# Attention followed by two gated layers: reciprocals fetched by two transfers of 64 partitions, tails of Q and K loaded per batch, zero columns beside the last keys, a new operation list

## The chip, the core and the metric

The kernel runs on one core of a Trainium2 chip. The metric is the device time of one execution in microseconds (us). Each engine (PE for matmuls, ACT, DVE and POOL for elementwise work) works off its own queue in order; SP issues nearly all DMAs, also in order. Engines wait for one another by semaphores.

## What is computed

```python
scores = scale * q @ k.T                     # 4 batches x 8 heads, 576 rows, head_dim 64
cum = cumsum(max(s, 0))
bias = min(-(cum[:, None] - cum[None, :]), 0)
attn = exp(where(causal, -1e9, scores + bias) - max)
x = (attn / (attn.sum(-1) + 1e-9)) @ v       # -> [2304 tokens, 512]
x = (sigmoid(x @ w_gate) * (x @ w_val)) @ w_out      # d_ff 1536
h = x @ w_in;  out = (h * cos(h)) @ w_out2           # d_ff 2048
```

## The kernel before

The heads go through in 16 pairs p = 0..15, four pairs j to a batch. The operations of a pair have short names, and the text `SEQ` at the top of the file lists all operations of all pairs in one order; `plan.run(SEQ)` walks through the list, picks buffers by planned times and emits each operation on its engine, so the order in `SEQ` is the order in each engine's queue. A letter behind a colon picks the engine (a ACT, d DVE, p POOL).

- GQ, GK, GV load Q, K (512 rows of each head, L515) and V (L574); GQT, GKT load the last 64 rows (L522, L525). Before the change GQT and GKT run for every second pair and bring the tails of two pairs (four heads) into the one buffer `Qt` or `Kt`, the other half of whose partitions was set to zero at the start.
- PQ, PK transpose them on PE (L546); HQ, HK copy the result to SBUF.
- DB brings the cumulated sums of a pair to all partitions (`CB`, L554, 576 KB). ZT, ZA, Z, ZM on POOL set masked biases.
- A are score matmuls (L618, L623), X adds the bias and takes the row maximum on DVE (L654), E is the exponential on ACT (L658), T transposes the result on PE (L444), C copies it (`pt`), V is the product with V on PE (L728, L730), U copies that to `w` (L433 or L437).
- The denominators take another way. RA adds 1e-9 on POOL (L737), RC takes the reciprocal on DVE (L740), RT transposes it on PE, RR copies it to `rr`, RD stores it to DRAM by two small DMAs (L749, L750), RB reads it back spread over all partitions into `rb` (L753, 288 KB), M multiplies `w` by `rb` (L759), XH and XL split the product in two parts for the next stage (L771). There is one `rb` and one `rr`: RB of a pair waits for M of the pair before it.
- w0, w1, w2 decode the first weight pieces; I0 to I7 are the first gate and value matmuls of the next stage.

Behind the list, `moe()` runs the two layers on PE without a break. Its first work on PE is gate and value of the second token block (needs only early batches), then the first down projection, which waits for `gh` on ACT (L826 sigmoid, L829). The memory of `tm` and `gh` is that of the attention's tiles, so these wait until the attention's last operations, XL of pair 15 among them, are through.

```python
def spread(u, p=p):                                              # RB, L753
    u.dma_start(out=RBT, in_=rec_d[p].unsqueeze(1).to_broadcast([2, 64, S]))
add(f"RB{p}", {"sp": 0.62}, spread, rd=[("rec", p)], wr=[rb], xfer=0.9)
```

Of the kernel before, what the change touches and what calls it, by code (L numbers as in the profile page):

```python
# [170 lines left out]
GQ0 cum tail B0 B1 GK0 GQT0 GKT0 out PQ0 table GK1 GQ1 BC0:d BC1:a Z0.0:p PK0 ZM0.3.0 HK0:a HQ0:d PK1 ZT0.0 Z1.0:a A3.0 DB1 ZT1.0 X0.3.0 ZA1.0 ZM1.3.0 ZA0.0 X1.3.0 HK1:a  # L171
PQ1 A4.0 ZM1.2.0 A0.0 GK2 A2.0 ZM0.2.0 HQ1:a ZT1.1 GK3 E0.3.0 GQ2 A4.1 X1.1.0 ZT0.1 X1.0.0 ZA1.1 X0.0.0 ZA0.1 Z1.1:p E1.3.0 Z0.1:p GQ3 X0.1.0 X1.2.0 ZM1.3.1 E1.1.0 X0.2.0
ZM0.3.1 E1.0.0 A0.1 E0.0.0 T0.0.0 E0.1.0 X1.0.1 T0.1.0 X1.1.1 X0.0.1 E1.2.0 X0.1.1 C0.1.0:d C0.0.0:a E0.1.1 A5.0 E0.0.1 A3.1 T0.3.0 GKT2 E1.0.1 X0.4.0 E1.1.1 T1.3.0 GQT2
T0.0.1 E0.4.0 X0.3.1 X1.3.1 T0.1.1 C0.0.1:a PK2 C0.3.0:a HK2:a ZM1.2.1 C1.3.0:d ZM0.2.1 A5.1 C0.1.1:d DB2 E0.2.0 T0.4.0 PQ2 ZT1.2 PK3 GV1 X0.4.1 A2.1 HQ2:a PQ3 GV0 E0.4.1
C0.4.0:d HQ3:a ZA1.2 T0.2.0 HK3:d ZT0.2 T1.2.0 A4.2 T0.4.1 X0.2.1 X1.2.1 A0.2 C0.4.1:d GQ4 ZA0.2 X1.0.2 C0.2.0:a Z1.2:p GQ6 X0.1.2 C1.2.0:a A3.2 E0.3.1 E1.3.1 E1.2.1 RA0
E1.0.2 T0.3.1 ZM1.3.2 X1.1.2 E0.1.2 Z0.2:p T1.3.1 X0.0.2 DB3 E0.2.1 X1.3.2 C1.3.1:a ZM0.3.2 C0.3.1:d RC0 GKT4 GK4 Z0.3:p V0.0 V1.0 T0.2.1 E0.0.2 X0.3.2 ZM1.2.2 E1.1.2
ZM0.3.3 T0.1.2 T0.0.2 T1.2.1 U0:a A5.2 Z1.3:p C0.0.2:d C0.2.1:d C0.1.2:a A2.2 C1.2.1:a ZT0.3 PK4 ZT1.3 A3.3 X0.4.2 X1.2.2 E0.3.2 GQT4 E1.3.2 ZM1.3.3 T0.3.2 ZM0.2.2 X0.2.2
HK4:a T1.3.2 GK5 ZA0.3 C1.3.2:a RT0 X0.3.3 E1.2.2 DB4 V0.1 ZM0.2.3 RR0:d V1.1 RA1 C0.3.2:d E0.4.2 T0.4.2 PQ4 X1.3.3 RC1 ZM1.2.3 RD0 ZA1.3 A4.3 U1:d HQ4:d GK6 A0.3 GV2
E0.2.2 ZT1.4 X1.0.3 X0.0.3 X0.1.3 E0.3.3 Z0.4:p E1.3.3 GV4 RT1 C0.4.2:a ZT0.4 RR1:a Z1.4:p ZA1.4 E1.0.3 E0.0.3 E0.1.3 A2.3 T0.2.2 ZA0.4 X1.1.3 T1.2.2 X0.2.3 A3.4 X1.2.3
RA2 E1.1.3 ZM1.3.4 C1.2.2:a RB0 T0.0.3 T0.1.3 A5.3 RC2 C0.0.3:a C0.2.2:d ZM0.3.4 C0.1.3:a PK5 RD1 HK5:a GQ5 X0.3.4 DB5 M0:p X0.4.3 warm0 RT2 T0.3.3 T1.3.3 RR2:d RB1  # L180
X1.3.4 A4.4 E0.4.3 C0.3.3:a C1.3.3:a ZM0.2.4 RD2 E1.2.3 T0.4.3 Z0.5:p A0.4 Z1.5:p E0.2.3 C0.4.3:d PQ5 X0.0.4 X1.0.4 X1.1.4 V0.2 GKT6 X0.1.4 V1.2 ZT1.5 HQ5:d T0.2.3 RA3
E1.0.4 ZT0.5 E1.3.4 XH0:p E1.1.4 E0.3.4 A2.4 E0.1.4 T1.2.3 U2:a E0.0.4 RC3 C1.2.3:a T0.1.4 C0.2.3:d X0.2.4 C0.1.4:a ZM0.3.5 T0.0.4 ZM1.2.4 A5.4 T0.3.4 GQT6 C0.0.4:a
# [37 lines left out]
def kernel(  # L220
# [168 lines left out]
    def attention():  # L389
        with ExitStack() as c2:  # L390
# [671 lines left out]
```

## Time and profile before

| | us |
|---|---|
| median of 3 runs (lowest, highest) | 1097.45 (1096.66, 1099.25) |
| the profiled execution | 1097.39 |
| its span, first to last instruction | 1095.5 |
| PE busy in the span | 1032.2 (94%) |
| DVE, ACT, POOL busy | 706.5, 477.8, 406.6 |

In slices of a fortieth of the span (27.4 us) the page shows PE at 7 to 8 tenths in the attention, and at 9 or more from the tenth slice on; the granted clock of PE is 8 to 9 tenths in the attention and full after it. The mean busy share of the 16 DMA engines is 3 to 6 tenths in the attention, then 1 to 2. A busy share is an average; what a change is worth is read from the waits of the stage it touches.

### The profile page before, as it was taken

Reading aid. Unit: us, or ns where it says so; the run is one execution under the profiler, and the core shown is the slowest. Engines: PE = TensorE matmul, PEld = TensorE weight load, DVE = VectorE, ACT = ScalarE, POOL = GpSimd, SP = SyncE. Lnnn points to the kernel's source line nnn. Section 1 sums busy time; section 2 is a strip of 40 time slices with the busy share of each in tenths; the row PEclk is TensorE's granted clock in tenths of the full one; section 3 lists DMA queues with packets and bytes.
Section 4 is the critical chain, followed back from the end, with each engine's and each line's share of the span. In section 5 each row is a group of like instructions: output and inputs, shape, how many; then the busy total and the mean of one; then the engine's idle time right before and its main releaser. Section 6 shows DMA issues by size and latency. Waiting matters only on the chain.

```text
span 1095.5 us, 17441 instructions
## 1 busy us (share of the span) xinstructions
PE 1032.2 (94%) x6554; PEld 932.9 (85%) x6554; DVE 706.5 (64%) x1366; ACT 477.8 (44%) x1079; POOL 406.6 (37%) x484
## 2 busy tenths in 40 slices
PE   8778768859999999999999999999999999999998
PEld 5555445539999999999999999999999999999997
DVE  5656546536665564775434488898778978885664
ACT  5757657614422221222212134566555555555443
POOL 3345545424322122232111122465435545453222
PEclk9989888978999999999999999999999999999999
DMA  6645445303211111111101012111101101100111
GB/s 165 158 120 160 131 117 147 82 31 103 71 39 48 50 39 39 59 61 55 39 21 39 20 58 58 40 58 58 39 20 59 58 20 42 56 20 1 58 51 65
DMA packets 93668, 69.94 MB, mean 64 GB/s; under 512 B 61008, under 2 KB 81872, under 8 KB 93584
## 3 DMA queue, kind: packets, MB, share of 16 engines
q1 hardware_dynamic: 92192, 68.43, 21.6%
q8 instruction: 51, 0.84, 0.3%
q10 hardware_dynamic: 1392, 0.40, 0.2%
q14 instruction: 33, 0.27, 0.1%
HBM read 63.95 MB, written 4.87 MB: 63 GB/s over the span
## 4 chain that ended last, share of the span: by engine, by line
PE 77%; DVE 0%; ACT 0%; DVEq 0%; issue 0%
PE pw L356 20%; PE pw L355 20%; PE pw L357 20%; PE pw L909 6%; PE pw L911 6%; PE pw L910 6%; DVE acc L927 0%; ACT gh L829 0%; DVEq L1057 0%
## 5 line engine op out<-in xcount | busy, mean ns | idle before, releaser
L355 PE MATMUL pw<-XH,wp 128*128 128x384 f32 x960 | 322.9, 336 | 1.0 <-DVE w L437 1.0
L357 PE MATMUL pw<-XH,wp 128*128 128x384 f32 x960 | 322.7, 336 | 0.0
L356 PE MATMUL pw<-XL,wp 128*128 128x384 f32 x960 | 322.7, 336 | 0.0
L310 POOL TENSOR_TENSOR wp<-wm,wp 128x512 fp32r<-128x512 f32 x68 | 100.9, 1485 | 228.9 <-DVE wp L309 226.3
L355 PEld LDWEIGHTS pw<-XH,wp 128*128 128x128 f32 x960 | 180.3, 188 | 5.3 <-DVE w L437 1.1
L356 PEld LDWEIGHTS pw<-XL,wp 128*128 128x128 f32 x960 | 180.1, 188 | 3.6
L357 PEld LDWEIGHTS pw<-XH,wp 128*128 128x128 f32 x960 | 180.1, 188 | 0.0
L899 POOL TENSOR_TENSOR gl<-tm,gh 128x384 fp32r<-128x384 f32 x96 | 109.2, 1137 | 143.8 <-ACT gh L898 143.7
L302 POOL TENSOR_TENSOR wm<-wm,wx 128x512 int32<-128x512 int32 x68 | 90.3, 1328 | 188.6 <-DVE wm L301 182.3
L827 DVE TENSOR_TENSOR tm<-pw,tm 128x384 f32<-128x384 f32 x72 | 40.1, 557 | 150.7 <-PE pw L357 139.1
L909 PE MATMUL pw<-wp,gh 128*128 128x512 f32 x288 | 112.2, 389 | 0.0
L910 PE MATMUL pw<-wp,gh 128*128 128x512 f32 x288 | 112.1, 389 | 0.0
L911 PE MATMUL pw<-wp,gl 128*128 128x512 f32 x288 | 112.1, 389 | 0.0
L355 PE MATMUL pw<-gh,wp 128*128 128x384 f32 x288 | 97.5, 339 | 7.9 <-ACT gh L829 7.9
L884 DVE SCALAR_TENSOR_TENSOR tm<-tm 128x384 f32<-128x384 int32 x96 | 98.2, 1023 | 3.3
L829 ACT CAST gh<-tm 128x384 fp32r<-128x384 f32 x72 | 37.0, 514 | 140.8 <-DVE tm L827 139.9
L356 PE MATMUL pw<-gl,wp 128*128 128x384 f32 x288 | 97.8, 340 | 0.0
L885 ACT ACTIVATE tm<-tm 128x384 f32<-128x384 f32 x96 | 50.5, 526 | 108.0 <-DVE tm L884 108.0
L357 PE MATMUL pw<-gh,wp 128*128 128x384 f32 x288 | 96.9, 337 | 0.0
L289 ACT ACTIVATE wx<-wx,ebias 128x512 int32<-128x512 int32 x68 | 49.2, 723 | 105.5 <-DVE wx L288 104.3
L658 ACT ACTIVATE pu<-pu,nm 128x512 f32<-128x512 f32 (+4 forms) x144 | 83.0, 579 | 10.5 <-POOL pu L437 6.2
L826 ACT ACTIVATE tm<-pw 128x384 f32<-128x384 f32 x72 | 35.1, 487 | 111.8 <-PE pw L357 95.8
(100 smaller groups left out, 1673.4 us busy)
## 6 DMA issues: line engine op xcount, KB each, us to landing
raw<-in_moe_w_out_dram SPq DMA_DIRECT2D x28, 512.0 KB
CB<-cum_d SPq DMA_DIRECT2D x15, 576.0 KB
raw<-in_moe_w_in_dram SPq DMA_DIRECT2D x16, 512.0 KB
raw<-in_moe_w_gate_dram SPq DMA_DIRECT2D x12, 512.0 KB
raw<-in_moe_w_val_dram SPq DMA_DIRECT2D x12, 512.0 KB
VN<-in_v_dram SPq DMA_DIRECT2D x31, 160.0 KB
rb<-rec_d SPq DMA_DIRECT2D x16, 288.0 KB
out_dram<-acc SPq DMA_DIRECT2D x17, 256.0 KB
```

The source lines that it names most:

```text
L302: pool.tensor_tensor(m, m, st["x"], ALU.add)
L310: pool.tensor_tensor(w[:, 1], m, f(w[:, 0]), ALU.subtract)
L355: pe.matmul(ps, wh, xh, start=first, stop=False)
L356: pe.matmul(ps, wh, xl, start=False, stop=False)
L357: pe.matmul(ps, wl, xh, start=False, stop=last)
L658: act.activation(o, o, AF.Exp, bias=NMT[nm.slot][:, col:col + 1], scale=-1.0, accum_out=SUMS[sums.slot][:, col:col + 1])
L884: dve.scalar_tensor_tensor(r, kk, -TWO_PI_LO, r, ALU.mult, ALU.add)
L885: act.activation(r, r, AF.Sin, scale=0.5)
L899: pool.tensor_tensor(gl, g, f(gh), ALU.subtract)
L909: pe.matmul(ps, gh[:, ts], w[:, 0], start=it["first"], stop=False)
L910: pe.matmul(ps, gh[:, ts], w[:, 1], start=False, stop=False)
L911: pe.matmul(ps, gl[:, ts], w[:, 0], start=False, stop=it["last"])
```

## The change

- **Spread of the reciprocals.** RB issues two DMAs, one for each head of the pair, each from 576 numbers in DRAM to 64 partitions of `rb`. Before, one DMA with an outer dimension of 2 filled all 128.
- **Tails.** GQT and GKT run for the first pair of a batch and bring the tails of all eight heads; there are two buffers each. K's tails now stand in partitions 64 to 127, so that in the transposed K the last keys stand behind the others, not ahead of them.
- **Zero columns.** The probability tile of the last 64 query rows is 640 columns wide; columns 576 to 639 are set to zero once, so that T of that tile transposes five plain blocks of 128.
- **Start.** Six small warming matmuls (`warm0`) stand before the first real ones, six (`warm1`) behind the first transposes; before, both stood late in the list. The store of the cumulated sums on ACT's queue goes behind the activation table's load.
- **List.** `SEQ` is new throughout, and the planned durations are changed in some places (SP's part of RB from 0.62 to 1.16, T of the small tiles, and others). `moe()` is not touched.

```diff
-GQ0 cum tail B0 B1 GK0 GQT0 GKT0 out PQ0 table GK1 GQ1 BC0:d BC1:a Z0.0:p PK0 ...
+tail cum GQ0 warm0 GKT0 B1 B0 GQT0 PQ0 table GK0 out BC0:a BC1:a GQ1 ZT0.0 PK0 ...
-            QKT = {x: att.tile([P, 2, 2, D], F32, name=f"{x}t") for x in "QK"}
+            QKT = {x: [att.tile([P, PB, 2, D], F32, name=f"{x}t{i}") for i in range(2)] for x in "QK"}
-            PU.append([att.tile([P, S], F32, name=f"pu4{i}") for i in range(NPU[4])])
+            PU.append([att.tile([P, NQ * P], F32, name=f"pu4{i}") for i in range(NPU[4])])
...
-                for e in range(2):
-                    u.memset(QKT["Q"][half(1 - e), :, e], 0.0)
-                u.memset(QKT["K"][half(1)], 0.0)
+                for i in range(2):
+                    for e in range(2):
+                        u.memset(QKT["Q"][i][half(1 - e), :, e], 0.0)
+                    u.memset(QKT["K"][i][half(0)], 0.0)
+                for i in range(NPU[4]):
+                    u.memset(PU[4][i][:, S:NQ * P], 0.0)
...
-            add("out", "act:500", setup_out, rd=["cum"], wr=["cum_d"], xfer=0.2)
+            add("out", "act:400", setup_out, rd=["cum", "table"], wr=["cum_d"], xfer=0.2)
...
-                    if p % 2 == 0:
-                        def load_tail(u, x=x, src=src[b, 2 * j:2 * j + 4, NT4 * P:S]):
+                    if j == 0:
+                        def load_tail(u, x=x, src=src[b, :, NT4 * P:S], tb=tb):
...
-                                u.dma_start(out=QKT[x][half(e), :, e], in_=src[e:e + 3:2].rearrange("h p d -> p h d"))
+                                u.dma_start(out=QKT[x][tb.slot][half(e), :, e], in_=src[e::2].rearrange("h p d -> p h d"))
...
-                                        i = (TAIL + c * P) % S if t == NT4 else c * P
+                                        i = c * P
...
-                    u.dma_start(out=RBT, in_=rec_d[p].unsqueeze(1).to_broadcast([2, 64, S]))
+                    for e in range(2):
+                        u.dma_start(out=RBT[half(e)], in_=rec_d[p, e].unsqueeze(0).to_broadcast([64, S]))
...
-                add(f"RB{p}", {"sp": 0.62}, spread, rd=[("rec", p)], wr=[rb], xfer=0.9)
+                add(f"RB{p}", {"sp": 1.16}, spread, rd=[("rec", p)], wr=[rb], xfer=0.9)
```

How the instructions stand at two places. The first is SP's queue around the first RB. Before, from the loads of V ahead of it to the second RB:

```order
L574 DMA VN_85<-in_v_dram 128x5x64 x2
L753 DMA rb<-rec_d 128x1x576
L749 DMA rec_d<-rr 2x4x128
L750 DMA rec_d<-rr 2x1x64
L515 DMA Qn_87<-in_q_dram 128x4x64 x2
L554 DMA CB_84<-cum_d 128x2x576
L753 DMA rb<-rec_d 128x1x576
```

And now:

```order
L580 DMA VN_85<-in_v_dram 128x5x64 x2
L762 DMA rb<-rec_d 64x576 x2
L757 DMA rec_d<-rr 2x4x128
L758 DMA rec_d<-rr 2x1x64
L560 DMA CB_83<-cum_d 128x2x576
L521 DMA Qn_88<-in_q_dram 128x4x64 x2
L521 DMA Qn_87<-in_q_dram 128x4x64 x2
L762 DMA rb<-rec_d 64x576 x2
```

Each RB has become two rows of 64 partitions, and the loads between two RBs have moved; the stores of `rr` (RD) have kept their shape.

The second place is the end of the attention on ACT, from the last exponential to the first sigmoid of the next stage. Before:

```order
L658 ACTIVATE pu_106,sums_111<-pu_106,nm_114 128x576
L433 COPY pt_94<-pw 128x2x128 x2
L433 COPY pt_94<-pw 128x3x128
L433 COPY pt_94<-pw 128x4x128
L826 ACT_TABLE_LOAD
L826 ACTIVATE tm<-pw 128x384
L829 CAST gh<-tm 128x384
```

And now:

```order
L666 ACTIVATE pu_105,sums_113<-pu_105,nm_116 128x512
L433 COPY pt_96<-pw 128x3x128 x2
L433 COPY pt_96<-pw 128x4x128 x2
L433 COPY w_110<-pw 128x576
L433 CAST XH<-w_111 128x576
L835 ACT_TABLE_LOAD
L835 ACTIVATE tm<-pw 128x384
L838 CAST gh<-tm 128x384
```

U of pair 14 (`w_110`) and XH of pair 15 are now ACT's and stand ahead of the table load and the sigmoid; before, they were on DVE and POOL. XL of pair 14, M and XL of pair 15 are POOL's last three instructions of the attention now; before, M and XL of pair 15 were DVE's.

## Rows read from the trace of the kernel before

**Rows 1.** Windows by stage: length, busy PE, PEld, DVE, ACT, POOL; clock, DMA share, GB/s.
```profile
20.00:48.80 28.80, 26.90 (x356) 18.47 (x352) 20.39 (x65) 24.71 (x74) 11.97 (x39) 0.94 0.63 154
48.80:220.00 171.20, 130.89 (x1463) 87.76 (x1458) 92.87 (x293) 108.25 (x322) 86.17 (x179) 0.89 0.48 127
220.00:248.00 28.00, 13.43 (x77) 8.21 (x75) 10.17 (x18) 2.87 (x4) 8.32 (x8) 0.77 0.08 29
248.00:1095.50 847.50, 843.71 (x4560) 808.62 (x4560) 572.61 (x955) 332.52 (x658) 292.16 (x226) 1.00 0.15 47
```

**Rows 2.** Waits of PE, 20 to 220 us: total us, times, longest.
```profile
PE pw L546 <- DMA Qt<-in_q_dram: 7.1, 2, 4.3
PE pw L728 <- DMA VN<-in_v_dram: 5.5, 4, 2.9
PE pw L444 <- DVE rr L437: 5.1, 1, 5.1
PE pw L444 <- ACT rr L433: 4.8, 2, 4.6
PE pw L546 <- DMA Qn<-in_q_dram: 4.7, 1, 4.7
...
PE pw L546 <- DVE nm L654: 3.1, 2, 2.9
```

**Rows 3.** Windows: a load of CB (first), a load of rb (second).
```profile
191.00:193.20 2.20, 2.20 (x20) 0.90 (x18) 1.76 (x10) 2.20 (x11) 0.24 (x1) 1.00 0.75 276
235.00:241.50 6.50, 4.43 (x24) 4.11 (x24) 1.62 (x3) 0.00 (x0) 1.29 (x1) 1.00 0.12 45
```

**Rows 4.** Timeline: M of pair 13, RB and M of pair 15.
```profile
223.34 1.40 POOL L759 TENSOR_TENSOR w<-w,rb 128x576 f32<-128x576 f32 x1 [8.54 <-DMA rb<-rec_d]
...
233.63 0.50 SPq L753 DMA_DIRECT2D rb<-rec_d  x1
...
242.02 0.76 DVE L759 TENSOR_TENSOR w<-w,rb 128x576 f32<-128x576 f32 x1 [5.39 <-DMA rb<-rec_d]
```

**Rows 5.** Waits, 0 to 250 us: of POOL, and of SP's queue.
```profile
POOL w L759 <- DMA rb<-rec_d: 54.3, 12, 8.5
...
SPq L753 <- DMA rec_d<-rr: 20.0, 10, 5.6
```

**Rows 6.** Timeline: a store of rr and its waiter; an RB, the loads of Q behind it.
```profile
45.44 0.58 SPq L750 DMA_DIRECT2D rec_d<-rr  x1
...
54.18 0.28 DVE L437 COPY rr<-pw 9x128 f32<-9x128 f32 x1 [6.09 <-DMA rec_d<-rr]
...
70.39 0.56 SPq L753 DMA_DIRECT2D rb<-rec_d  x1
71.00 1.24 SPq L515 DMA_DIRECT2D Qn<-in_q_dram  x2
```

**Rows 7.** Lines of ACT (first), then timeline, from 226 us to the first down projection.
```profile
L433 ACT COPY w<-pw 128x576 f32<-128x576 f32 x5 | 3.1, 628 | 0.9 <-PE pw L730 0.9
...
226.19 0.28 PE L444 MATMUL pw<-ident,rc 64*9 64x64 f32 x2 [5.76 <-DVE rc L740]
...
228.82 1.28 ACT L826 ACT_TABLE_LOAD   x1
...
232.00 2.76 PE L730 MATMUL pw<-pt,VN 128*64 128x512 f32 x20
...
246.00 1.41 POOL L771 TENSOR_TENSOR XL<-w,XH 128x576 fp32r<-128x576 f32 x1
246.08 0.49 ACT L826 ACTIVATE tm<-pw 128x384 f32<-128x384 f32 x1 [15.97 <-POOL wp L310]
246.60 0.56 DVE L827 TENSOR_TENSOR tm<-pw,tm 128x384 f32<-128x384 f32 x1 [1.96 <-ACT tm L826]
...
247.44 0.51 ACT L829 CAST gh<-tm 128x384 fp32r<-128x384 f32 x1 [0.87 <-POOL XL L771]
...
248.00 0.69 PE L355 MATMUL pw<-gh,wp 128*128 128x384 f32 x1 [7.86 <-ACT gh L829]
```

More of the change, by code (lines that the diff above doesn't have):

```diff
@@ L213 @@
-M12:p I0 E0.0.15 X1.2.15 XH11:a X0.2.15 I1 E1.1.15 I2 RC14 RB13 E1.0.15 E0.1.15 T0.1.15 XH12:a M13:p E0.2.15 E1.2.15 RT14 RR14:d T0.0.15 A5.15 T0.4.14 XH13:p X0.4.15 I3
-C0.0.15:a I4 GV15 RD14 I5 E0.4.15 C0.4.14:d C0.1.15:a T0.4.15 T0.2.15 T1.2.15 T0.3.15 C1.2.15:d T1.3.15 C0.4.15:d C0.2.15:a I6 RA15 RB14 RC15 w2mant_hi I7 RT15 C1.3.15:d
-C0.3.15:a V0.14 V1.14 XL13:d RR15:d V0.15 w2mant_lo XL11:d V1.15 U14:d M14:d U15:d RD15 XL12:p XH14:d RB15 w2sign M15:d XH15:p XL15:d w2split XL14:p
+tail cum GQ0 warm0 GKT0 B1 B0 GQT0 PQ0 table GK0 out BC0:a BC1:a GQ1 ZT0.0 PK0 GK1 warm1 Z0.0:p HQ0:a ZT1.0 Z1.0:p DB1 ZM0.3.0 PQ1 ZA0.0 HK0:d A3.0 ZM1.3.0 ZA1.0 X0.3.0
@@ L416, in attention @@
             pl = {n: Pool(c) for n, c in dict(
-                Q=NQK, K=NQK, Qt=1, Kt=1, cc=NCC, vn=NV, pt=NPT, w=NW, rb=1, sums=3, nm=3, rc=1, rr=1, raw=1,
+                Q=NQK, K=NQK, Qt=2, Kt=2, cc=NCC, vn=NV, pt=NPT, w=NW, rb=1, sums=3, nm=3, rc=1, rr=1, raw=1,
                 cb=NCC, **{f"pu{t}": NPU[t] for t in range(NQ)},
@@ L447, in attention @@
             zero = PU[4][1].bitcast(BF16)[:, 0:512]
-            ss, cs, one = WT[0][0:NH], WT[1][0:NH], PU[4][0][0:NH]
+            ss, cs, one = WT[0][0:NH], WT[1][0:NH], PU[4][0][0:NH, 0:S]
             sp.dma_start(out=ss, in_=s.rearrange("b h s -> (b h) s"))
@@ L492, in warm @@
                         pe.matmul(PW[:, wm.slot, 0:2 * P], one_b[:, 0:P], one_b, start=z == 0, stop=z == 5)
-                add(f"warm{i}", "pe:650", warm, rd=["z"], wr=[wm, "z"], at=3.9)
+                if i == 0:
+                    add("warm0", "pe:1200", warm, wr=[wm, "begin"], at=3.9)
+                else:
+                    warm1 = warm, wm
             def geom(t):
@@ L544, in prep @@
                                     o = o[:, i:i + D]
[L545 removed]
+                                i = QKN[x][qk.slot][half(h), c] if c < NT4 else QKT[x][tb.slot][half(h), j]
                                 pe.transpose(o, i.rearrange("p e d -> p (e d)"), ident[half(h), half(h)])
[L547 removed]
+                    add(f"P{x}{p}", "pe:380", prep, rd=[(qk, 0), (qk, 1), tb] + ["begin"] * (p == 0), wr=[ps] + [("turned", x)] * (p == 0))
                     def keep(u, x=x, ps=ps, cc=cc):
@@ L555, in attention @@
                 if p:
-                    add(f"DB{p}", {"sp": 0.55}, spread_cum, rd=["cum_d"], wr=[(cb, e, 0) for e in range(2)], xfer=2.1)
+                    add(f"DB{p}", {"sp": 0.45}, spread_cum, rd=["cum_d"], wr=[(cb, e, 0) for e in range(2)], xfer=2.1)
                 else:
@@ L577, in attention @@
                 add(f"GV{p}", {"sp": 1.05}, load_v, rd=[], wr=[vn], xfer=1.4)
-                ready = [(cc, x) for x in "QK"]
+                if p == 0:
+                    add("warm1", "pe:700", warm1[0], rd=[("turned", x) for x in "QK"], wr=[warm1[1], "go"])
+                ready = [(cc, x) for x in "QK"] + ["go"] * (p == 0)
                 first, late = [], []
@@ L622, in scores4 @@
                             z = e ^ turn
-                            pe.matmul(PW[:, sc[0].slot + z, 0:HS], OPS["Q"][cc.slot][half(e), QCOL[NT4]:QCOL[NT4] + P], OPS["K"][cc.slot][half(e), z * HS:(z + 1) * HS], start=turn == 0, stop=turn == 1)
+                            pe.matmul(PW[:, sc[0].slot + z, 0:HS], OPS["Q"][cc.slot][half(e), QCOL[NT4]:QCOL[NT4] + P], OPS["K"][cc.slot][half(e), TAIL + z * HS:TAIL + (z + 1) * HS], start=turn == 0, stop=turn == 1)
                     groups[g] = ts, s4, pus, pu_of, sc, at, bias
@@ L627, in attention @@
                         parts = [lambda u, turn=turn, scores4=scores4: scores4(u, turn) for turn in range(2)]
-                        add(f"A4.{p}", "pe:480", parts[0], rd=ready, wr=[sc[0], ("a4", p)], needs=[pus[NT4][0]])
+                        add(f"A4.{p}", "pe:500", parts[0], rd=ready, wr=[sc[0], ("a4", p)], needs=[pus[NT4][0]])
                         sc4 = sc[0]
                     else:
-                        add(f"A{g}.{p}", f"pe:{ {0: 660, 2: 640, 3: 850}[g] }", scores, rd=ready + [("a3" if g == 2 else "a4", p)] * (g != 3), wr=sc[:1] + ([("a3", p)] if g == 3 else [("a0", p)] if g == 0 else []), needs=[pus[t][0] for t in ts])
+                        add(f"A{g}.{p}", f"pe:{ {0: 720, 2: 670, 3: 870}[g] }", scores, rd=ready + [("a3" if g == 2 else "a4", p)] * (g != 3), wr=sc[:1] + ([("a3", p)] if g == 3 else [("a0", p)] if g == 0 else []), needs=[pus[t][0] for t in ts])
                 for e in range(2):
@@ L635, in bias4_tail @@
                     def bias4_tail(u, e=e, cb=cb, pu=pu):
-                        later(u, PU[NT4][pu.slot][half(e), 0:TAIL], CB[cb.slot][:, e][half(e), NT4 * P:S])
+                        later(u, PU[NT4][pu.slot][half(e), NT4 * P:S], CB[cb.slot][half(e), e, NT4 * P:S])
                     def bias4(u, e=e, cb=cb, pu=pu):
-                        copy(u, PU[NT4][pu.slot][half(e), TAIL:S], CB[cb.slot][half(e), e, 0:NT4 * P])
+                        copy(u, PU[NT4][pu.slot][half(e), 0:NT4 * P], CB[cb.slot][half(e), e, 0:NT4 * P])
                     add(f"ZT{e}.{p}", "pool:180", bias4_tail, rd=[(cb, e, 0)], wr=[(pu, e, "t"), ("z4", p, e)])
                     add(f"ZA{e}.{p}", "pool:490", first[e], rd=[(cb, e, 0), ("z4", p, e)], wr=[(cb, e, 2)])
-                    add(f"Z{e}.{p}", "pool:562 act:470", bias4, rd=[(cb, e, 0)], wr=[(pu, e, "c"), ("z5", p, e)])
+                    add(f"Z{e}.{p}", "pool:562 act:640", bias4, rd=[(cb, e, 0)], wr=[(pu, e, "c"), ("z5", p, e)])
                 for g, (ts, s4, pus, pu_of, sc, at, bias) in ((g, groups[g]) for g in (3, 2, 0, 4)):
```

104 lines of the change are left out of this document (52 added, 52 removed).

## The prediction

> **What bounds the kernel now.** I read the windows by stage first. From 248.0 us on, PE is busy for 843.7 of 847.5 us at full clock [rows 1]: the two layers are bound by PE, the change doesn't touch them, and they should take the same 847.5 us from the moment when their first down projection starts (248.00, [rows 7]). So the question is when that start comes. The profiled execution took 1097.4 us, 1.9 more than its span and 0.05 below the median of the runs, so a shift of the start is taken off 1097.4 as it stands.
>
> Ahead of that start lie three stretches. From 20 to 48.8 us, before the first reciprocals have come in, PE is busy 26.90 of 28.80 us at a granted clock of 0.94 and works off 356 matmuls, 12.4 per us. From 48.8 to 220 it is busy 130.9 of 171.2 us at 0.89, 8.5 matmuls per us. From 220 to 248 it is busy 13.4 of 28 [rows 1]. So PE has 40 us of idle time in the second stretch and 14.6 in the third, and no other engine fills it: ACT is busy 108, DVE 93, POOL 86 of the 171 us.
>
> PE's waits name the late ones: loads of Q's tail, of V and Q, the copy of the transposed reciprocals (DVE rr, ACT rr) and once a row maximum, 30.3 us in six rows [rows 2]. Behind all of them I see the read-back of the reciprocals. POOL waits for `rb` 54.3 us in 12 places [rows 5]. While an `rb` comes in, the 16 DMA engines are busy to 0.12 and move 45 GB/s, for 6.5 us; a load of CB, twice the bytes, runs at 0.75 and 276 GB/s in 2.2 us [rows 3]. A share of 0.12 is 2 engines of 16. What is issued right behind an RB and also needs those two engines stands in line there: a store of 0.5 KB issued at 45.44, just after the first RB, is still awaited by DVE at 54.18, and in those 6 us PE and DVE stand still together; the loads of Q that PE waited 4.7 us for were issued at 71.00, just behind the RB at 70.39 [rows 2, 6].
>
> In the last stretch the same transfer stands on the path itself. M of pair 13 waits 8.54 us for its `rb`; behind it in POOL's queue stands RA of pair 15, so RC, RT and the products with V on PE start only at 226.2, after a wait of 5.8. RB of pair 15 is issued at 233.63, M follows at 242.02, 8.4 us later, and the down projection at 248.00 after PE idled 7.86 us [rows 4, 7].
>
> **The change part by part.** *Spread.* Each half has an outer dimension of 64, where the old one had 2; the load of CB, with 128 partitions outside, shows what such a shape does [rows 3]. At 276 GB/s the 288 KB take 1.1 us instead of 6.5. From RB to M 8.4 becomes 8.4 - 6.5 + 1.1 = 3.0, and 0.3 more for the second issue (0.5, [rows 4], partly beside the first's way): 3.3. The Trainium skill, page "DMA: Bandwidth & Descriptors", section on why a DMA increments its semaphore by 16, states that a DMA uses the largest number of engines up to 16 that divides the slowest dimension of both sides; by it the old shape gets 2 and each new half 16, and the trace agrees with the 2 (0.12 busy). By the same rule the stores of `rr`, whose outer dimension stays 2, keep two engines.
>
> *Middle stretch, 171.2 us.* If `rb` no longer fills two engines, the six waits go: -30.3. PE is also slower after each idle stretch: clock 0.89 against 0.94 in the first means half speed (1.2 of 2.4 GHz) for 0.22 against 0.12 of the time, 17 us more, of which PE is busy three quarters; half of those 13 us is lost, -6.
>
> *What comes late next.* The new list moves every load, and the trace of before cannot show where one is late now. RD keeps its shape, and RB stands in SP's queue until RD has landed (20.0 us in 10 places, [rows 5]); all loads issued behind it wait with it. The three rows of waits for loads make 17.3 us; between 0 (all were caused by `rb`) and 17 I keep a little over half, as ACT would be busy 108 of some 135 us and collisions get more: +10, start included.
>
> *End.* Taken from the start of pair 14's product with V, since scores and exponentials of all pairs are through by then: that product 3.0 (2.76 and four small ones), U on ACT 0.63, M of pair 14 on DVE 0.76, which frees `rb`, RB to M 3.3, M of pair 15 on POOL 1.40, XH on ACT 0.63 (as U). Then XL on POOL (1.41) runs beside ACT's table load 1.28, sigmoid 0.49 and DVE's product 0.56, which are longer with 2.33; `gh` 0.51; handovers 0.7. In all 13.3 us where 28.0 pass now [rows 1, 4, 7]: -14.7. Pair 15's product with V and the next block's matmuls lie beside it. The table load, before this done at 228.82 in idle time, is now behind XH and costs 0.9 of the 13.3 (2.33 less 1.41); the end is shorter all the same.
>
> *Start, tails, zeros.* `warm0` and `warm1` move six small matmuls each to the front, where PE waits for loads anyway; both were in the list before. Loading tails per batch saves 4 issues for K and 8 for Q on SP, of some 0.6 us each (the store in rows 6 takes 0.58), 7 us; the second half of RB adds 16 times 0.5, 8 us. SP's time is even, between -1 and +2. The zero columns cost two memsets on POOL in the first microseconds, while it waits for sums; T and the score matmuls keep count and shape. I set these at 0, bounds -2 and +2.
>
> *Sum:* 1097.4 - 30.3 - 6 - 14.7 + 10 = 1056.4, say **1056**. Alone, with the late loads between 0 and 17 and the end between 9 and 15, it is 1046 to 1069.
>
> **Rivals.** *The next engine limits (A).* ACT, DVE and POOL each have their queue in order, and with PE's gaps closed ACT would be at 80%. If the new list only brings back half of the 51 us (30.3 + 6 + 14.7), the time is 1072. For: POOL is busy 0.50 in the middle stretch and only 0.42 in the first, whose pace I take as proof [rows 1]; M, XH and XL come on top. Against: ACT's share in that first stretch is 0.86, and it held PE up little. *PE's pace of the first stretch holds (B).* 1463 matmuls at 12.4 per us take 118 us instead of 171, so -53, with the end -14.7: 1030. For: it was reached with DMA engines at 0.63. Against: the mix lacks U, M and the weight decoding. *Fixed time counts twice (C).* What an RB takes beyond its transfer is 8.4 - 6.5 = 1.9 us; if the second half begins only after the first has landed, 16 times 1.9 is 30 on top of the forecast, 1086. Against: pairs of loads of Q are issued in 1.24 us together [rows 6]. The Trainium skill, the same page, section "Bandwidth", wants transfers batched to 1 MiB, and its fit gives each DMA about 2.0 us fixed; by it 16 more DMAs in a row would cost about 32 us (an estimate), 1088; no run here shows yet whether two halves overlap. *The halves are not spread (D).* They stay on two engines, 0.12 busy, and the list alone moves little: 1097 to 1099. *Slower (E).* The halves are not spread and RB lies on the path in all pairs, as that of pair 15 does now: 16 second issues of 0.5 are +8, and the end gains ACT's table load 1.3 and M on POOL, 1.40 for 0.76: 1107. It decides if the DMA share beside an RB stays near 0.12.
>
> **How the numbers follow.** Forecast 0.62, A 0.18, B 0.11, C 0.04, D 0.02, E 0.03. The range 1040 to 1078 takes in the forecast's own bounds, the nearer half of A and the nearest part of B; a tenth lies beyond each end. A measurement of this kernel tells about 0.2% (2.2 us) from no change: faster 0.95 (forecast, A, B, C), same 0.02 (D), slower 0.03 (E).
>
> **What would show it.** Right: beside an RB the DMA share well above 0.12; 3 to 3.5 us from the last RB to its M; POOL's wait for `rb` below 15 us in all; no wait of DVE or ACT rr over 2 us; the first down projection at 205 to 210 us and 847.5 us after it. Wrong: the share unchanged (D, E); M late though `rb` has landed early, with ACT or POOL at 85% and over (A); waits of PE for Q, V or tails of more than 12 us in sum though `rb` is quick, which would put the fault on RD or SP's order; a change in the 847.5.

## The result

| | before | after |
|---|---|---|
| median (lowest, highest), us | 1097.06 (1096.62, 1099.25) | 1039.01 (1037.40, 1042.41) |
| ratio, 95% interval | | 0.947 [0.944, 0.950] |
| profiled execution, its span, us | 1097.39, 1095.5 | 1042.41, 1040.6 |
| first down projection starts, us | 248.00 | 193.43 |
| PE busy in the span, us (matmuls) | 1032.2 (6554) | 1014.0 (6554) |

The change makes the kernel 5.3% faster. The forecast was 1056 us with a range from 1040 to 1078: the direction was right, the gain too small, 41 us where 58 came, and the median lies 1 us below the range. The whole difference lies ahead of the first down projection; the layers behind it take 847.2 us (before 847.5).

### The profile after

Windows by stage of the changed kernel, cut at the start of pair 14's product with V (178.2) and at the first down projection (193.4); columns as in [rows 1]:

```profile
20.00:48.80 28.80, 26.72 (x370) 17.59 (x366) 22.09 (x67) 24.77 (x75) 13.17 (x40) 1.00 0.72 171
48.80:178.20 129.40, 115.18 (x1438) 73.24 (x1438) 94.15 (x303) 107.58 (x318) 86.14 (x179) 0.99 0.65 166
178.20:193.40 15.20, 10.33 (x73) 7.05 (x72) 7.51 (x11) 3.60 (x5) 8.17 (x6) 1.00 0.17 45
193.40:1040.60 847.20, 843.10 (x4560) 808.49 (x4560) 572.58 (x955) 332.68 (x658) 292.45 (x226) 1.00 0.15 47
```

The kernel before, cut at the same two places of the program (its pair 14 starts its product at 226.4):

```profile
48.80:226.40 177.60, 131.53 (x1466) 88.00 (x1460) 93.45 (x295) 108.25 (x322) 89.00 (x183) 0.89 0.47 123
226.40:248.00 21.60, 12.79 (x74) 7.98 (x72) 9.59 (x16) 2.87 (x4) 5.49 (x5) 0.74 0.08 28
```

The middle went from 177.6 to 129.4 us. Of these 48.2 us, PE's idle time gave 31.9 (46.1 to 14.2), and its busy time gave 16.3 (131.5 to 115.2) for nearly the same number of matmuls, at a granted clock of 0.99 in place of 0.89. The end went from 21.6 to 15.2.

The other engines' busy times in the middle are almost unchanged (ACT 108.3 and 107.6, DVE 93.5 and 94.2), so what went was waiting. The three longest waits of PE from 20 to 178 us (total, times, longest), of POOL for `rb` and of SP's queue for the store of `rr` (both 0 to 200 us):

```profile
PE pw L444 <- ACT pt L433: 6.4, 8, 3.5
PE pw L444 <- ACT pu L666: 1.8, 3, 0.7
PE pw L444 <- DVE nm L662: 1.3, 2, 1.1
```

```profile
POOL w L768 <- DMA rb<-rec_d: 8.6, 6, 2.4
```

```profile
SPq L762 <- DMA rec_d<-rr: 6.2, 8, 1.1
```

No wait of PE for a load is left in this profile (in that of the same kernel run again, experiment 5, 2.4 us for Q and K); the rows for Q, its tail, V and `rr` of [rows 2] are gone. POOL's wait for `rb` fell from 54.3 to 8.6 us, SP's wait for the store of `rr`, whose shape did not change, from 20.0 to 6.2 [rows 5].

Windows of 2 us beside two spreads, of pair 14 and of pair 15:

```profile
179.20:181.20 2.00, 2.00 (x22) 1.13 (x18) 0.81 (x2) 0.00 (x0) 1.97 (x2) 1.00 0.58 150
185.70:187.70 2.00, 1.05 (x9) 0.98 (x7) 1.42 (x2) 0.00 (x0) 0.78 (x1) 1.00 0.47 148
```

The same 288 KB are in within 2 us, at a DMA share near a half, where the old ones took 6.5 us at 0.12 [rows 3]. The Trainium skill, page "DMA: Bandwidth & Descriptors", section on why a DMA increments its semaphore by 16, gives the old shape 2 engines and each new half 16. The traces agree with the 2 (a share of 0.12, 45 GB/s) and show many more for the halves (about 0.5 and 150 GB/s, in a window that may be longer than the transfer); that it is just 16 they do not show.

The end, from the timeline (start, length, engine, line, operation, in brackets the idle time before):

```profile
178.41 2.76 PE L738 MATMUL pw<-pt,VN 128*64 128x512 f32 x20
...
181.28 0.64 ACT L433 COPY w<-pw 128x576 f32<-128x576 f32 x1 [3.51 <-PE pw L738]
...
182.09 0.81 DVE L437 COPY pt<-pw 128x640 f32<-128x640 f32 x1
182.82 1.01 DVE L437 CAST XH<-w 128x576 fp32r<-128x576 f32 x1
...
183.76 0.74 DVE L768 TENSOR_TENSOR w<-w,rb 128x576 f32<-128x576 f32 x1
...
184.53 1.13 SPq L762 DMA_DIRECT2D rb<-rec_d  x2
...
188.12 1.42 POOL L768 TENSOR_TENSOR w<-w,rb 128x576 f32<-128x576 f32 x1 [1.64 <-DMA rb<-rec_d]
189.57 0.67 ACT L433 CAST XH<-w 128x576 fp32r<-128x576 f32 x1 [7.66 <-POOL w L768]
190.26 1.28 ACT L835 ACT_TABLE_LOAD   x1
...
192.86 0.51 ACT L838 CAST gh<-tm 128x384 fp32r<-128x384 f32 x1 [0.82 <-issue]
...
193.43 0.44 PE L355 MATMUL pw<-gh,wp 128*128 128x384 f32 x1 [2.28 <-ACT gh L838]
```

From the issue of the last RB (184.53) to its M (188.12) pass 3.6 us, forecast 3.3, before 8.4 [rows 4]. M of pair 14 starts at 183.76, though its input was copied by 181.92: it stands in DVE's queue behind a copy of `pt` and XH of pair 13, 1.84 us. The table load lies on the path, as the prediction said.

One thing must be known to compare single profiles. In some executions PE's clock rises to its upper level at 4 to 6 us, in others only at 12.5 to 14, for the same kernel. The clock column reads 1.00 ahead of that first rise in both cases, but the matmuls tell. The first eight of a form, in the changed kernel's profile and in that of its repetition (grouped lines, 0 to 20 us: busy, mean ns):

```profile
L569 PE MATMUL pw<-w,ident 32*128 32x288 f32 x8 | 4.2, 702 | 0.0
```

```profile
L569 PE MATMUL pw<-w,ident 32*128 32x288 f32 x8 | 2.3, 427 | 0.0
```

The repetition's first down projection came at 188.73, 4.7 us earlier. That the early rise alone makes this difference is not shown: the kernel of experiment 1 has a profile of each kind too (698 and 411 ns), and its first down projection came at 190.07 and 189.81, 0.3 us apart. The profiles of before (699 ns) and of after are both of the late kind, so they may be compared as they stand.

### The profile page after: what moved, and what is told of

It reads as the page before. It is cut to its first block, busy times and chain, and to the rows that moved or that the text cites. A ratio compares the mean times of both kernels' runs of the same rounds, so it can differ in the third digit from the quotient of the medians.

```text
span 1040.6 us, 17428 instructions
## 1 busy us (share of the span) xinstructions
PE 1014.0 (97%) x6554; PEld 917.6 (88%) x6554; DVE 704.6 (68%) x1366; ACT 477.9 (46%) x1079; POOL 410.4 (39%) x489
## 4 chain that ended last, share of the span: by engine, by line
PE 81%; DVE 0%; ACT 0%; issue 0%; DVEq 0%; ACTq 0%
PE pw L356 21%; PE pw L357 21%; PE pw L355 21%; PE pw L918 6%; PE pw L919 6%; PE pw L920 6%; DVE acc L936 0%; DVE gl L844 0%; ACT gh L838 0%; ACT tm L835 0%; DVEq L1066 0%; ACTq L838 0%
## 5 line engine op out<-in xcount | busy, mean ns | idle before, releaser
L666 ACT ACTIVATE pu<-pu,nm 128x576 f32<-128x576 f32 (+4 forms) x144 | 83.3, 581 | 5.4 <-DVE nm L662 5.4
L901 DVE SCALAR_TENSOR_TENSOR tm<-tm,pw 128x384 f32<-128x384 f32 x96 | 52.8, 550 | 42.4 <-ACT tm L895 42.4
```

Source lines behind the costliest of these rows:

```text
L666: act.activation(o, o, AF.Exp, bias=NMT[nm.slot][:, col:col + 1], scale=-1.0, accum_out=SUMS[sums.slot][:, col:col + 1])
L901: dve.scalar_tensor_tensor(g, r, -0.5, h, ALU.add, ALU.mult)
```

## The experiments

The ratios are to the kernel before, run on the same chip beside it.

### 1. The spread alone

```diff
 # kernel before
-                    u.dma_start(out=RBT, in_=rec_d[p].unsqueeze(1).to_broadcast([2, 64, S]))
+                    for e in range(2):
+                        u.dma_start(out=RBT[half(e)], in_=rec_d[p, e].unsqueeze(0).to_broadcast([64, S]))
```

> The kernel before, its list and everything else unchanged, only the spread of the reciprocals as two DMAs of 64 partitions. Theory S (the two-engine transfer is the cause: it is late itself and holds up every load behind it): the six waits of PE (30.3 us) shrink below 10, POOL's wait for rb from 54.3 to under 20, the half-clock time shrinks with them; 1045 to 1062 us, that is most of the 58. Rival L (the new list is the cause, the old one was poor): within 12 us of before, 1085 to 1097.

Measured: 1041.82 us (1040.01 to 1044.48), ratio 0.950 [0.947, 0.953], 3 us below the range expected of theory S; rival L is out. PE waits for no load from 20 to 178 us, and POOL's wait for `rb` is 9.7 us. Its middle and end, cut as above:

```profile
48.80:175.40 126.60, 117.08 (x1444) 76.31 (x1440) 90.96 (x293) 106.81 (x318) 87.66 (x181) 0.99 0.68 171
175.40:190.10 14.70, 10.05 (x75) 6.95 (x73) 8.70 (x15) 2.87 (x4) 4.58 (x4) 1.00 0.10 24
```

Three lines, with the old list, tails and zeros, give 55 of the 58 us. 126.6 us for the middle is even a little less than in the changed kernel. It also bears on a rule that stood against the change: the Trainium skill, the same page, section "Bandwidth", wants transfers batched to 1 MiB. With the fixed 2.0 us per DMA that the Trainium skill fits on this page (section on the anatomy of one DMA, for DMAs issued by GpSimd, while SP issues these), the prediction had 1088 us as a rival, an estimate. Here 16 more and smaller DMAs took 55 us off. By the DMA shares beside the two forms (0.12, about 0.5), what decided was on how many engines each lay.

### 2. Everything but the spread

```diff
 # kernel after
-                    for e in range(2):
-                        u.dma_start(out=RBT[half(e)], in_=rec_d[p, e].unsqueeze(0).to_broadcast([64, S]))
+                    u.dma_start(out=RBT, in_=rec_d[p].unsqueeze(1).to_broadcast([2, 64, S]))
```

> The changed kernel with the old spread, one DMA with an outer dimension of 2. Theory S: DMA share near 0.12 beside an RB, POOL waits 40 us or more for rb, loads behind an RB late again, the clock at half speed for tens of us; 1085 to 1105 us. Rival L: under 1055. A third reading, that the list only pays together with the quick spread, gives e1 in the middle (1065 to 1075) and e2 near 1097.

Measured: 1080.91 us (1079.29 to 1082.06), ratio 0.985 [0.983, 0.988]. That is 4 us below the range of theory S, and 26 above that of rival L; the third reading is out with experiment 1. POOL waits 35.1 us for `rb` in the whole attention, where 40 or more were expected. The longest wait of PE and of POOL, 20 to 226 us:

```profile
PE pw L552 <- DMA Qn<-in_q_dram: 8.6, 2, 4.6
```

```profile
POOL w L767 <- DMA rb<-rec_d: 28.4, 9, 6.5
```

With the slow spread, list, tails and zeros are worth 16 us; with the quick one only about 3 (experiment 1 against the result). So the two gains overlap. That with the new list fewer operations stand behind the slow transfer is the likely reading, and was not tested. Between this kernel and the changed one only the shape of the spread differs, and it makes 42 us.

### 3. The two engines filled again, for nothing

```diff
 # kernel after
+            RBX = att.tile([P, S], F32, name="rbx")
...
                     for e in range(2):
                         u.dma_start(out=RBT[half(e)], in_=rec_d[p, e].unsqueeze(0).to_broadcast([64, S]))
+                    if p < NP - 2:
+                        u.dma_start(out=RBX, in_=rec_d[p].unsqueeze(1).to_broadcast([2, 64, S]))
```

> The changed kernel, and behind each pair's two DMAs a third of the old shape (outer dimension 2, 288 KB) to a tile that nobody reads, for pairs 0 to 13. The reciprocals themselves come as early as in the changed kernel; only what queues on the two engines is late. If the cost before lay in the loads and stores that stood behind rb: 1060 to 1085 us, with PE waiting for Q, V or tails and DVE or ACT rr for stores, and little waiting of POOL for rb. If it lay in rb's own lateness: 1037 to 1048.

Measured: 1087.76 us (1086.89 to 1088.67), ratio 0.991 [0.989, 0.994], 3 us more than the most that was expected. Nobody reads the third transfer. The waits that came back, 20 to 226 us, of PE, DVE, ACT and POOL, and of SP's queue (0 to 250 us):

```profile
PE pw L553 <- DMA Qn<-in_q_dram: 14.7, 3, 6.3
PE pw L737 <- DMA VN<-in_v_dram: 7.5, 5, 3.5
```

```profile
DVE rr L438 <- DMA rec_d<-rr: 11.4, 3, 5.6
```

```profile
ACT rr L434 <- DMA rec_d<-rr: 9.8, 2, 7.1
```

```profile
POOL pu L466 <- DMA CB<-cum_d: 28.3, 7, 8.5
POOL pu L438 <- DMA CB<-cum_d: 24.5, 5, 6.2
```

```profile
SPq L763 <- DMA rec_d<-rr: 21.8, 7, 8.5
```

POOL's wait for `rb` itself stays at 9.2 us in 6 places (0 to 250 us). So 49 of the 58 us are lost again although POOL waits for `rb` hardly longer than in the changed kernel (8.6): the loss is that of the other transfers. One of them, from the timeline:

```profile
95.25 0.54 SPq L765 DMA_DIRECT2D rbx<-rec_d  x1
...
95.90 0.40 SPq L561 DMA_DIRECT2D CB<-cum_d  x1
...
106.57 0.23 POOL L466 TENSOR_SCALAR_AFFINE_SELECT pu<-CB 64x64 f32<-64x64 f32 x1 [5.43 <-DMA CB<-cum_d]
```

A load of CB issued right behind the third transfer is awaited until 10.7 us after its issue; such a load ran in a window of 2.2 us [rows 3]. SP's queue waits 21.8 us again for the store of `rr` (6.2 in the changed kernel), and the loads issued behind it stand there with it. How the 49 us divide between these two ways is not shown. Nor was a third transfer of the quick shape run, which would tell what fourteen more DMAs cost by their count and bytes; the twelve smaller ones of experiment 7 cost 7 us at most.

### 4. More work for PE

```diff
 # kernel after, in turn()
+                    one_b = ident.bitcast(BF16)
+                    for z in range(6):
+                        pe.matmul(PW[:, rt.slot, 0:2 * P], one_b[:, 0:P], one_b, start=z == 0, stop=z == 5)
```

> The changed kernel with six more small warming matmuls (128 columns moved of a 128x128 block, as in warm0) on PE in each pair, before the transposes of the reciprocals. Six of them take 0.8 us in the profile, 16 times 0.8 is 13. If PE sets the pace of the attention in the changed kernel: +9 to +13 us, 1048 to 1053. If ACT or the queues' order sets it: under +5.

Measured: 1042.54 us (1041.41 to 1046.15), ratio 0.951 [0.948, 0.953], 3.5 us above the changed kernel. Its windows from 48.8 to 178.2 us:

```profile
48.80:178.20 129.40, 119.85 (x1474) 76.53 (x1472) 91.92 (x301) 104.45 (x310) 84.32 (x177) 1.00 0.65 167
```

PE's busy time up to the first down projection grew by 9 us (170.9 to 180.1), the time by less than half of that. PE alone does not set the pace of the middle. ACT, the next one, is busy 107.6 of 129.4 us in the changed kernel; more work on it was not tried.

### 5. The changed kernel and the spread alone, again

Both kernels of experiment 1 and of the result, unchanged, side by side on one chip, since their difference is small.

> The changed kernel as it is, timed beside the next one on one chip, to tell the spread alone from the whole change. Theory N (the rest of the change, list and tails and warming, is worth nothing once the spread is quick): 1037 to 1042, within 2 us of the spread alone. Rival R (the rest is worth a few us): 3 us or more below it.

> The kernel before with only the spread changed, again. Theory N: 1037 to 1042, intervals that overlap with the changed kernel's. Rival R: 1041 to 1045, intervals apart.

Measured: 1038.24 us (1037.43 to 1043.16), ratio 0.948 [0.945, 0.950], and 1044.20 us (1040.05 to 1045.64), ratio 0.951 [0.949, 0.954]. The rest of the change is worth 3 to 6 us by the medians of the two pairs of runs; the intervals overlap, so that it is above zero is likely, not shown.

### 6. Fewer warming matmuls

```diff
 # kernel after, warm0 and warm1
-                    for z in range(6):
-                        pe.matmul(PW[:, wm.slot, 0:2 * P], one_b[:, 0:P], one_b, start=z == 0, stop=z == 5)
+                    for z in range(1):
+                        pe.matmul(PW[:, wm.slot, 0:2 * P], one_b[:, 0:P], one_b, start=True, stop=True)
```

> The changed kernel with one matmul in the place of six in each of warm0 and warm1. If the warming holds up the clock in the first stretch: the first transposes and scores run at half speed, 2 to 5 us more and half-clock time before 20 us. If it is idle filler: same within 1.5 us.

Measured: 1041.38 us (1037.09 to 1042.21), ratio 0.949 [0.946, 0.951]. Windows of the first 10 us:

```profile
0.00:10.00 10.00, 8.06 (x48) 4.63 (x50) 3.50 (x8) 3.75 (x6) 5.92 (x24) 0.88 0.76 156
```

The clock falls once in the first 20 us, from 7.63 to 11.05. The median is 3.1 us above that of the changed kernel on the same chip (experiment 5), outside the 1.5 us of idle filler and inside the 2 to 5 of the other reading, but the intervals overlap and the time moves by less than the runs of one kernel differ: this experiment does not decide between the two. Here the first rise came early, at 4.2 us, with one warming matmul, while the changed kernel with six has both kinds. What sets the moment of the rise stays open.

### 7. The tails in twice the DMAs

```diff
 # kernel after, load_tail(); K's tail alike
                             for e in range(2):
-                                u.dma_start(out=QKT[x][tb.slot][half(e), :, e], in_=src[e::2].rearrange("h p d -> p h d"))
+                                for z in range(2):
+                                    u.dma_start(out=QKT[x][tb.slot][half(e), 2 * z:2 * z + 2, e], in_=src[4 * z + e:4 * z + 4:2].rearrange("h p d -> p h d"))
```

> The changed kernel with each load of the last 64 rows of Q and K cut into two by heads: the bytes are the same, twelve more DMAs are issued in all. It puts a price on the part of the change that loads these rows once per batch instead of once per pair. Theory: what a DMA costs here is what it holds up on the 16 engines, and these loads lie beside a queue that has room (SP and ACT wait in the first stretch for nothing that PE waits for), so the time stays within 2 us of the changed kernel's 1038 to 1039 us. Rival: the count of DMAs is itself what the loads cost; twelve issues more, on the queues that feed the first pairs, delay the first pairs and the time becomes 1043 to 1047 us, and PE waits for Qn or Kn show up in the first 60 us.

Measured: 1045.49 us (1044.29 to 1048.35), ratio 0.952 [0.950, 0.953]. Every run lies above the eight of the changed kernel; the difference is 4 to 5 us by the ratios, 6 to 7 by the medians. My expectation of no change fell: the rival's time came. But its place was another. From 20 to 48.8 us PE is busy 26.66 us as against 26.72, so the first pairs lose nothing. POOL's waits for the loads of CB grow from 9.8 to 19.7 us (0 to 200 us, of the changed kernel and of this one):

```profile
POOL pu L465 <- DMA CB<-cum_d: 8.7, 4, 3.6
...
POOL pu L437 <- DMA CB<-cum_d: 1.1, 2, 0.7
```

```profile
POOL pu L465 <- DMA CB<-cum_d: 11.8, 6, 3.7
...
POOL pu L437 <- DMA CB<-cum_d: 7.9, 3, 3.2
```

The first down projection comes at 198.46, 5.0 us later (the clock's first rise is late in both profiles). Of these, 4.3 us are PE's busy time for the same matmuls (170.9 to 175.3): PE is at half speed for 14.0 us after the first rise, in the changed kernel for 3.4. The first of these stretches begins at 119.6, while PE waits 2.84 us for a row maximum, shortly after POOL waited for CB; four score matmuls then take 2.08 us, which take 1.13 in the changed kernel. So late loads of CB, idle PE and a fallen clock fit as a chain, but it was not tested, and CB alone is not enough: with two buffers for `rb` (experiment 9) POOL waits 16.6 us for CB, and the kernel is faster. The kernel before issues its tails in this same number of DMAs, so loading them once per batch can account for all that the change gains beyond the spread.

### 8. Three buffers for `rr` in the kernel before

```diff
 # kernel before; copy and store use RRT[rr.slot]
-            RRT = att.tile([NS, P], F32, name="rr")
+            RRT = [att.tile([NS, P], F32, name=f"rr{i}") for i in range(3)]
```

> The kernel before, with its one spread DMA, but three buffers for rr (the turned reciprocals) instead of one, so that the turning copy of a pair no longer waits until the store of the pair before it has landed. In the kernel before DVE waited 6.1 us and ACT 8.3 us for that store. Theory (the old spread's 0.12 share of the engines holds up loads, stores and the spread itself alike): the wait only moves to the next late transfer, to rb and to the loads of Q; gain 0 to 6 us, 1091 to 1097 us. Rival (the one buffer of rr was the main damage, through the in-order queues of DVE and ACT): 10 to 14 us gain, 1083 to 1087 us, and the PE waits behind it go.

Measured: 1095.38 us (1093.76 to 1097.49), ratio 0.998 [0.997, 0.999]. The waits for the store of `rr` (6.1 us of DVE, 8.3 of ACT in the kernel before) are gone; PE's longest, 20 to 226 us, are now:

```profile
PE pw L546 <- DMA Qt<-in_q_dram: 9.7, 3, 4.4
PE pw L546 <- DMA Qn<-in_q_dram: 8.4, 2, 5.0
PE pw L546 <- DVE nm L654: 7.9, 1, 7.9
```

The first down projection still comes at 248.03. 14 us of waits went and 2 us of time: as long as the cause stays, one late transfer takes the place of another.

### 9. A better end

The first kernel gives `rb` two buffers and puts M, XH and XL of the last pair on DVE; the other two do one of these each.

```diff
 # kernel after
-            RBT = att.tile([P, S], F32, name="rb")
+            RBT = [att.tile([P, S], F32, name=f"rb{i}") for i in range(2)]
...
-w2split U14:a C0.4.15:d V0.15 XH13:d M14:d RD15 XH14:d XL14:p RB15 V1.15 U15:d XL13:d M15:p XH15:a XL15:p
+w2split U14:a C0.4.15:d V0.15 XH13:d M14:d RD15 XH14:d XL14:p RB15 V1.15 U15:d XL13:d M15:d XH15:d XL15:d
```

> The changed kernel with M, XH and XL of pair 15 on DVE (0.76, 0.46, 0.76 us in the profile, for 1.42 on POOL, 0.67 on ACT, 1.42 on POOL), so that ACT's table load and sigmoid no longer stand behind XH, and with two buffers for rb, so that the last RB need not wait for M of pair 14. From the last product's end: 2.0 us from the shorter steps, 1.4 from the earlier rb; the first down projection at about 190 instead of 193.4, 1034 to 1038 us. If the down projection waits for something else there (memory, weights): same as the changed kernel.

> The changed kernel with two buffers for rb and nothing else: one half of the run that beat it (e7, 1032.7 us, which also moves M, XH and XL of the last pair to DVE). It tells whether the transfer still limits after it is quick. Theory: in the changed kernel POOL still waits 8.6 us for rb in six places and the spread of a pair is issued only when M of the pair before has freed the one buffer; with two, RB is issued right behind RD, those waits go to below 4 us, and the last stretch (from pair 14's product with V to the first down projection) falls by 1 to 2 us from 15.2; time 1034 to 1037. Rival: the buffer no longer matters once rb comes in 3.5 us, and the gain of e7 is that of the engine at the end: 1037 to 1040.

> The changed kernel with M, XH and XL of the last pair on DVE instead of POOL, ACT and POOL, and one rb buffer: the other half of the run that beat it (1032.7 us). M takes 0.75 us on DVE instead of 1.42, XL 0.75 instead of 1.42, and ACT can do its table load early. Theory: the last stretch falls by 1.5 to 2.5 us from 15.2 and nothing ahead of it changes, 1036 to 1038. Rival (the end alone made the gain of e7, 6 us): 1032 to 1035.

Measured, in this order: 1032.73 us (1030.75 to 1035.57), ratio 0.943 [0.941, 0.945]; 1035.64 (1032.81 to 1038.60), 0.944 [0.941, 0.947]; 1038.11 (1036.84 to 1038.85), 0.946 [0.944, 0.948]. By the medians, the first lies 1 us below its expected range, the second inside and the third at its upper end; neither half's rival came. The timeline of the first at its end:

```profile
173.00 1.13 SPq L762 DMA_DIRECT2D rb<-rec_d  x2
...
178.48 0.75 DVE L768 TENSOR_TENSOR w<-w,rb 128x576 f32<-128x576 f32 x1
...
179.76 0.76 DVE L780 TENSOR_TENSOR XL<-w,XH 128x576 fp32r<-128x576 f32 x1
...
181.14 0.51 ACT L838 CAST gh<-tm 128x384 fp32r<-128x384 f32 x1 [5.87 <-DVE tm L836]
```

The last RB is issued at 173.00 and M follows at 178.48, when its other input is there: the transfer is off the path. From pair 14's product with V to the first down projection pass 12.8 us with both, 14.3 with the two buffers, 13.2 with DVE, 15.2 in the changed kernel. So both halves shorten the end, by 0.9 us (1 to 2 expected) and 2.0 (1.5 to 2.5). POOL's waits for `rb` did not go below 4 us with two buffers: 5.8 us are left. In whole times the buffers seem worth 3 us, DVE less than can be told from none, and both 6; these steps are as large as the spread of a kernel's runs, and only the 6 is beyond the intervals. The kernel with both beats the one before and the changed one.

## Why the prediction came out too small

**What bounds the kernel, and the mechanism: right.** The old spread on two engines was the cause, and what it cost was mostly the time of other transfers. Experiment 1 takes it away and has nearly the whole gain, experiment 3 puts the load back and loses most of it, with `rb` itself in time.

**The sum, on one cut.** The forecast counted its new end (13.3) from pair 14's product with V, but the 28.0 us that it replaced from 220, 6.4 us ahead of that product. This does not alter its sum; put where they belong, the terms are:

| step | forecast, us | measured, us |
|---|---|---|
| middle, PE's idle time: six waits -30.3, the 6.4 before pair 14's product, late loads +10 | -26.7 | -31.9 |
| middle, PE's busy time (clock) | -6 | -16.3 |
| end: 21.6 to 13.3 | -8.3 | -6.4 (to 15.2) |
| layers behind | 0 | -0.3 |
| sum | -41.0 | -54.9 |

The profiled execution fell by 55.0 (1097.39 to 1042.41); that of experiment 5 is 4.8 us lower. The bounds given for the forecast alone, 1046 to 1069, do not follow from its terms: with late loads of 0 to 17 and an end of 9 to 15 they are 1042 to 1065, and the median lies below these too.

**The step that failed most: the clock, 10 of the 14 us.** The prediction compared the middle with the first stretch (0.89 with 0.94) and took half of what PE is busy in 17 us. But the first stretch was no measure of undisturbed PE: after the change it runs at 1.00 itself, and the middle at 0.99. From the clock's first rise to the first down projection, half-speed stretches sum up to 53.6 us in the kernel before and 3.4 in the changed one; with the quick spread alone to 3.5, with the old spread in the new list to 38.1, with the third transfer to 47.8. Score matmuls of one form, and a product with V (grouped lines, 48.8 to 178 us: busy, mean ns), before and after:

```profile
L618 PE MATMUL pw<-K,Q 64*128 64x512 f32 x36 | 13.2, 784 | 0.7 <-DVE pt L437 0.7
...
L730 PE MATMUL pw<-pt,VN 128*64 128x448 f32 x36 | 8.4, 539 | 0.0
```

```profile
L626 PE MATMUL pw<-K,Q 64*128 64x512 f32 x48 | 13.7, 644 | 0.7 <-ACT pt L433 0.4 <-DVE nm L662 0.2
...
L738 PE MATMUL pw<-pt,VN 128*64 128x448 f32 x48 | 11.1, 539 | 0.0
```

Not all matmuls got cheaper there: most scores and the transposes of Q and K did, the products with V hardly. Up to the first down projection PE's busy time fell from 188.5 to 170.9 us for the same matmuls. A better estimate could have been had from the rows of before: a granted clock of 0.89 means half speed for 0.22 of 171 us, 38 us [rows 1]; PE was busy about three quarters of that, 28 us, and at full speed this work takes half, so -14; the window of after holds 28 matmuls fewer, which is about the rest of the 16.3. The prediction had subtracted the first stretch's 0.12 as if that would stay. The split into busy and idle time is exact as a sum; what the clock alone would give is not shown, for in experiment 4 an added 9 us of busy PE cost 3.5 us of time.

**Late loads, +10: failed the other way.** The prediction kept a little over half of the 17.3 us of load waits. None was left: with the spread alone, under the old list, the waits for Q's tail, V and Q are gone as well (0 and 0.6 us in its two profiles), so all hung on the old spread. Experiment 3 brings two of the three back. This is worth 5 us of the sum, with the small waits between engines that took part of their place.

**The end: 1.9 us too good.** RB to M was right to 0.3 us. What was left out is DVE's queue: M of pair 14 waits 1.84 us there behind a copy and XH of pair 13, and RB waits for M.

**Start, tails, zeros at 0 with 2 either way: a little too small.** The whole rest of the change is worth 3 to 6 us with the quick spread. The tails, costed by SP's issue time alone, are the likely part: experiment 7 gives twelve DMAs more of this kind 4 to 7 us.

**Rivals.** Half the gain (A, 1072), fixed time twice (C, 1086), no spreading (D) and slower (E) are out. The pace of the first stretch (B, 1030) was the nearer one: 1438 matmuls in 129.4 us are 11.1 per us, against its 12.4 and the old 8.5. It was given 0.11, and the lower end of the range, 1040, took too little of it in. What spoke against it (U, M and the decoding of weights come on top) may be why the pace stayed below its 12.4; experiment 4 shows that PE had some room.

## What to carry to other kernels

When a transfer occupies few of the DMA engines (a share near 0.12 while it runs, 45 GB/s), look for what stands in line behind it, not only for who waits for it: here 49 of 58 us were lost again with a transfer that nobody reads, and curing one waiter moved 14 us of waits for 2 us of time. Where PE idles in many short pieces, price the clock with the rest: every matmul at half speed counts, and the measure is full speed, not the best stretch of the slow kernel. For work moved to an engine in the last stretch, list what its queue holds at that moment; 1.8 us of the end lay there.

## What was not expected

- The same 288 KB, in two halves, leave PE at most 2.4 us of waits for loads (experiment 5), while a store of 0.5 KB behind the old form was still awaited over 8 us after its issue [rows 6].
- Twelve more loads, beside some two hundred DMAs of the attention, cost 4 to 7 us with the same bytes.
- The moment when PE's clock first rises differs from run to run of one kernel, 4 to 6 or 12.5 to 14 us from the start, and the clock column doesn't show it; the changed kernel run again was 4.7 us earlier at the first down projection with the early rise, the spread alone 0.3 us. Between six warming matmuls and one the times don't decide.
- 96 more matmuls (9 us of busy PE) cost 3.5 us. In that profile the half-speed stretches between the first rise and the first down projection were gone altogether, but so they were in experiment 5 without these matmuls.
